# Up's product P6 in two levels beside P5, VectorE's sums regrouped, and k's decay head by head on ScalarE

## The chip, the cores and the metric

The kernel runs on one core of one Trainium2 chip. The metric is the device time of one execution in microseconds (us), the median of several runs. The engines are TensorE (PE: matmuls, PEld: their weight loads), VectorE (DVE), ScalarE (ACT), GpSimd (POOL) and SyncE (SP). POOL and SP issue the transfers here. Each engine works through its own list of instructions in a fixed order, and waits where the next one needs something that is not there yet.

## The reference

```python
for b in range(nb):                    # blocks of 64 positions
    intra = (q_b @ k_b^T * Dmask) @ v_b
    inter = (q_b * lam_pow) @ kv_state
    out[b] = intra + inter
    kv_state = lam**64 * kv_state + (k_b * rev_pow)^T @ v_b
x = out as (3072, 512)                 # (B*S, H*D)
h = x @ w_in                           # (3072, 2048), "Up"
y = (h - tanh(h)) @ w_out              # (3072, 512), "Down"
```

q, k and v are (4, 8, 768, 64), lam has a value per head; everything is float32.

## The kernel before

The kernel takes positions in blocks of 128 and works in six groups (g = 0 to 5). A group is one block of all four batches: 512 tokens. For each group it does attention, then Up (512 to 2048), then Down (2048 to 512). The attention of group g+1 is put between the products of Down of group g.

**Strassen's scheme.** From group 1 on, Up and Down are multiplied by Winograd's form of Strassen's scheme: a matrix product in 2 x 2 quarters takes seven products P1 to P7 of quarters or of sums of quarters (S1 to S4 of the left factor, T1 to T4 of the right one) in place of eight. FACT names the factors: P1 = A11 B11, P2 = A12 B21, P3 = S4 B22, P4 = A22 T4, P5 = S1 T1, P6 = S2 T2, P7 = S3 T3. Each of these may itself be split the same way: "in two levels". Then it is seven products of sixteenths, in the order STEPS = 1, 2, 6, 5, 7, 3, 4.

**Up.** Left factors are weights: w1[u] (quarters and S3) and ws[u] (S1, S2, S4), for u = 0 to 3, each u being 512 of the 2048 columns. up (L540 to L583) does one product for one u in one level: four matmuls of 128x256 (L553). From group GI = 2 on P1, P2 and P5 are done in two levels by inner_steps (L623 to L652): per step four matmuls of 128x128 (L637), one for each u. The right factors' sums come from inner_tokens (L611 to L619, on VectorE at L618), the weights' sums from inner_weights (L601 to L609), which writes them to the DRAM tensor fine_in in group 1; they are read back in pieces of 256 KB. In a two-level product the bank y gathers steps 1, 6, 7 and 4, and is copied out after each of them (L641 by ScalarE, L648 by VectorE), so the next step on y waits for the copy. Steps 5 and 3 share the bank z (L646 copies after step 5), step 2 has w; L651 adds them.

In the up stage, for each u, a bank y is seeded with P1's result by ScalarE (seed, L526 to L529), P6 (L553) is added to it, and it is copied to hidden part 12 (L570); then P7 goes into y (VectorE adds it to part 22 at L574), and P4 last, so y is the sum for part 21. A bank z is seeded with P5's result, and P3 is added to it (L579). finish (L559 to L562) takes the tanh on ScalarE (L561) and subtracts it on VectorE (L562). L582 and L583 make the sums S1 and S3 of Down's left factor, first_sum (L585 to L591) finishes part 11.

**Down.** down_twice (L797 to L841) does a product of Down in two levels: seven steps of four 128x128 matmuls (L811), whose weights come in pieces from the DRAM tensor fine. POOL's queue reads these pieces (L696, and L693 for fine_in) in the order of stream into RING = 7 buffers, so a read waits until TensorE has used the piece seven places earlier. sums_twice (L787 to L795, the operations at L794) makes the left sums on VectorE, L817 the last of them. Copies are at L815 (ScalarE), L824 and L825 (VectorE). sums_once makes Down's S2 (part 11 = S1 - part 11, L739).

**Attention.** att_transpose (L362, L373) works from blocks on VectorE; att_scores (L387, L389, masks L393 on VectorE); att_read (L433), the state's decay on ScalarE (L437); kv_products (L408), which needs k decayed by att_decay (L397 to L399: one VectorE multiplication of 128x512 per batch); att_out (L462, L473, copies L484 on ScalarE, state's addition L482 on VectorE). k itself is loaded by SP (L159) into three buffers.

**Order of a group g >= 2** (L1028 to L1141): the up stage (u = 0 to 3) with Down's P1 spread between; Down's P2; the first half of attention g+1; P4, P5, P6 of Down; the second half; P7; then P3 of Down in turn with P1 and P2 of the next group's Up, then P5 of Up, and P6 for u = 0 and 1. P6 for u = 2 and 3 lies in the up stage. The order written in the source is not yet the order on the engines: a scheduler moves instructions, except where tied or keep_in_program_order holds them.

## Time and profile before

| what | value |
|---|---|
| three runs, median (lowest to highest) | 651.78 us (649.89 to 652.12) |
| the profiled execution, its own time | 650.99 us |
| its span, first to last instruction | 649.2 us |
| matmul records on PE | 6080 |
| P6's first L553 block in groups 2, 3, 4 and 5, by the chain | 269.05, 370.71, 472.09, 572.45 us |
| transfers | 135.79 MB, 209 GB/s over the span |

The profile is of one execution. Times in it are in us from the span's start, durations of single instructions in ns or us as marked. "Idle before" is the time for which an engine waited ahead of the instruction, and the name behind the arrow is what ended the wait. Records of matmuls overlap: the pitch from one to the next, not the duration, is what a matmul costs TensorE. The differences in the row on P6's first block, 101.7, 101.4 and 100.4 us, are the time of a whole group.

### The profile page before, as it was taken

Reading aid. Unit: us, or ns where it says so; the run is one execution under the profiler, and the core shown is the slowest. Engines: PE = TensorE matmul, PEld = TensorE weight load, DVE = VectorE, ACT = ScalarE, POOL = GpSimd, SP = SyncE. Lnnn points to the kernel's source line nnn. Section 1 sums busy time; section 2 is a strip of 40 time slices with the busy share of each in tenths; the row PEclk is TensorE's granted clock in tenths of the full one; section 3 lists DMA queues with packets and bytes.
Section 4 is the critical chain, followed back from the end, with each engine's and each line's share of the span. In section 5 each row is a group of like instructions: output and inputs, shape, how many; then the busy total and the mean of one; then the engine's idle time right before and its main releaser. Section 6 shows DMA issues by size and latency. Waiting matters only on the chain.

```text
span 649.2 us, 15718 instructions
## 1 busy us (share of the span) xinstructions
PE 641.8 (99%) x6080; PEld 594.7 (92%) x6080; DVE 499.2 (77%) x969; ACT 250.2 (39%) x513; POOL 242.6 (37%) x418
## 2 busy tenths in 40 slices
PE   8999999999999999999999999999999999999998
PEld 7888888888888999989999989999998999998997
DVE  4467989958999895778986678998477997485873
ACT  3686765523221222543223453213453313264210
POOL 6000136767756335203435302443411354411341
PEclk9999999999999999999999999999999999999999
DMA  9869987988979858958757967775967686712575
GB/s 201 214 168 206 247 244 233 382 252 231 276 191 268 242 181 253 220 118 220 247 174 226 248 134 160 230 253 199 237 140 158 199 274 210 233 67 66 159 247 162
DMA packets 160281, 135.79 MB, mean 209 GB/s; under 512 B 128640, under 2 KB 130944, under 8 KB 160208
## 3 DMA queue, kind: packets, MB, share of 16 engines
q0 software_dynamic: 30496, 97.88, 47.8%
q1 hardware_dynamic: 128096, 36.53, 26.6%
q8 instruction: 48, 0.79, 0.5%
q10 hardware_dynamic: 1616, 0.39, 0.3%
q14 instruction: 25, 0.20, 0.1%
HBM read 110.10 MB, written 24.64 MB: 208 GB/s over the span
## 4 chain that ended last, share of the span: by engine, by line
PE 91%; DVE 4%; DMA 2%; ACT 1%; issue 1%; ACTq 0%; SPq 0%; DVEq 0%
PE y L811 17%; PE y L553 17%; PE zw L811 13%; PE h L870 8%; PE y L637 7%; PE z L553 6%; PE acc L900 4%; PE z L637 3%; DMA k_nat<-in_k_dram 2%; PE sp L387 2%; PE op L462 2%; PE w L637 2%; PE kv L408 1%; PE op L433 1%; PE end L856 1%; PE op L473 1%
## 5 line engine op out<-in xcount | busy, mean ns | idle before, releaser
L696 POOL DMA_DIRECT2D wb<-fine x204 | 110.1, 540 | 244.0 <-PE y L811 160.8
L815 ACT ACTIVATE q<-y 128x128 f32<-128x128 f32 x112 | 31.1, 277 | 143.2 <-PE y L811 141.7
L811 PE MATMUL y<-wb,g 128*128 128x128 f32 x584 | 76.5, 277 | 0.2 <-DVE tt L618 0.2
L811 PEld LDWEIGHTS y<-wb,g 128*128 128x128 f32 x584 | 70.5, 192 | 1.2 <-issue 0.4
L870 PE MATMUL h<-xt,w 128*128 128x256 f32 x256 | 57.8, 382 | 0.4 <-DVE w L325 0.4
L870 PEld LDWEIGHTS h<-xt,w 128*128 128x128 f32 x256 | 47.6, 190 | 7.8 <-DVE w L325 1.1
L811 PE MATMUL zw<-wb,g 128*128 128x128 f32 x368 | 48.9, 276 | 0.0
L561 ACT ACTIVATE th<-g 128x512 f32<-128x512 f32 x40 | 25.2, 630 | 59.9 <-DVE g L579 42.2
L562 DVE TENSOR_TENSOR g<-g,th 128x512 f32<-128x512 f32 x40 | 27.7, 691 | 24.5 <-ACT th L561 24.4
L811 PEld LDWEIGHTS zw<-wb,g 128*128 128x128 f32 x368 | 44.8, 192 | 0.6 <-DVE g L817 0.6
L553 PE MATMUL y<-xt,w 128*128 128x256 f32 x192 | 45.0, 379 | 0.0
L553 PEld LDWEIGHTS y<-xt,w 128*128 128x128 f32 x192 | 36.4, 190 | 5.1 <-ACT g L570 0.2
L553 PE MATMUL z<-xt,ws 128*128 128x256 f32 x160 | 38.8, 381 | 0.1
L553 PE MATMUL y<-tt,w 128*128 128x256 f32 x160 | 38.3, 382 | 0.0
L811 PE MATMUL zw<-wb,s 128*128 128x128 f32 x280 | 37.9, 275 | 0.0
L553 PE MATMUL y<-tt,ws 128*128 128x256 f32 x160 | 37.8, 379 | 0.0
L811 PE MATMUL y<-wb,s 128*128 128x128 f32 x280 | 37.5, 277 | 0.0
L811 PEld LDWEIGHTS zw<-wb,s 128*128 128x128 f32 x280 | 35.2, 192 | 0.4
L811 PEld LDWEIGHTS y<-wb,s 128*128 128x128 f32 x280 | 34.7, 192 | 0.6
L553 PEld LDWEIGHTS y<-tt,w 128*128 128x128 f32 x160 | 29.8, 190 | 4.7 <-DVE g L574 0.5
L900 PE MATMUL acc<-wt,g 128*128 128x256 f32 x144 | 33.5, 382 | 0.4 <-DVE g L906 0.2
L553 PEld LDWEIGHTS y<-tt,ws 128*128 128x128 f32 x160 | 29.8, 190 | 3.7
(215 smaller groups left out, 1446.0 us busy)
## 6 DMA issues: line engine op xcount, KB each, us to landing
wb<-fine POOLq DMA_DIRECT2D x204, 256.0 KB, 3.8
wb<-fine_in POOLq DMA_DIRECT2D x36, 256.0 KB, 4.4
raw<-in_moe_w_out_dram SPq DMA_DIRECT2D x12, 512.0 KB, 6.2
rest<-fine POOLq DMA_DIRECT2D x20, 256.0 KB, 4.6
raw<-in_moe_w_in_dram SPq DMA_DIRECT2D x16, 256.0 KB, 6.2
fine<-f POOLq DMA_DIRECT2D x16, 256.0 KB, 4.8
q_blk<-in_q_dram SPq DMA_DIRECT2D x128, 32.0 KB, 3.4
k_blk<-in_k_dram SPq DMA_DIRECT2D x128, 32.0 KB, 3.5
```

Source lines behind the costliest of these rows:

```text
L387: tied(g != 1, nc.tensor.matmul(out=sp[j][ts(r, HALF), x:3 + p:2 + p - x, :], lhsT=k0, rhs=qj.rearrange("d (t i) -> d t i", t=2), start=Tr ...
L408: tied(g == 0, nc.tensor.matmul(out=kv[ts(j, 64), n, p, :], lhsT=kd[:, 2 * p + j, :], rhs=vn[:, 2 * p + j, :], start=n == 0 and p == 0, st ...
L462: tied(g == 0, nc.tensor.matmul(out=dst(n, p, j)[:, HALF:BLK], lhsT=vn[:, 2 * p + j, :], rhs=ss[:, j, 2 + p, :], start=g == 0 and n == 0 a ...
L553: nc.tensor.matmul(out=t[:, m, :], lhsT=wt[:, kt, ts(m, 128)], rhs=x[:, kt, :], start=first and m == 0 and kt == 0, stop=kt == 1, skip_gro ...
L561: nc.scalar.activation(th, src, AF.Tanh)
L562: nc.vector.tensor_tensor(dst(c), src, th, op=AL.subtract)
L637: nc.tensor.matmul(out=dst[:, ts(u, 128)], lhsT=a, rhs=b, start=x in (1, 2, 5) and u == 0, stop=True, skip_group_check=True)
L696: nc.gpsimd.dma_start(out=t.rearrange("p m c -> p (m c)"), in_=fine[TWICE.index(n_), SUB.index(x_)].rearrange("p u c -> p (u c)"))
L811: tied(x == STEPS[-1], nc.tensor.matmul(out=dst, lhsT=a[:, u, :], rhs=wb[:, ts(u, 128)], start=x in (1, 2) and u == 0, stop=u == NU - 1, s ...
L815: nc.scalar.activation(keep, dst, AF.Copy)
L870: tied(u == 0, nc.tensor.matmul(out=hm[c][:, m, :], lhsT=w1[u][:, i, a, ts(m, 128)], rhs=xt[0, t][:, i, :], start=m == 0 and i == 0, stop= ...
L900: nc.tensor.matmul(out=acc[n][:, r, :], lhsT=a[:, ts(r, 128)], rhs=b, start=kt == 0 and r == 0, stop=kt == KH - 1, skip_group_check=True)
```

## The change

P6 of Up joins P1, P2 and P5 in two levels (INNER has 6). The sums of its weights are made by 16 VectorE operations at the end of group 1 (inner_weights in the loop over STEPS, into the dead buffer of group 1's S1 part) and written to fine_in. Its tokens' sums are made in each group by inner_tokens. Its steps alternate with those of P5, its result lands in the hidden part 21 (dead at that time), and a new function second_sum adds it to P1's result on VectorE for each u; only then is y seeded. So the up stage has only P3, P7 and P4 left; the order of these is written anew, with the seeds of u = 2 and 3 behind P4 of u = 0 and 1, and L570 is not run any more from group 2 on.

In Down, S2 (sums_once(g, 11, ...)) and P1's sums are moved: S2 stands behind the first half of attention and P2's results (every(p2)), P1's sums behind up(0, 7). More operations are held in program order (L408, L433, L739 from group 2 on), fewer elsewhere (seeds and L641, L646).

att_decay from group 3 on is done by ScalarE: eight operations of 128x64 per batch, each with the head's column of the mask as a per-partition scale.

On the engines the scheduler makes this of it in groups 2 to 5, from the crossing on. TensorE: fourteen blocks of P5 and P6 in turn, two matmuls of Down's P1, P3 and P7 of u = 0, half of P7 of u = 1, then one matmul of P4 of u = 0, P3 of u = 1, and so on. VectorE: the four second sums, then 36 operations up to the last P4's subtraction; behind P2's and P4's sums come the four masks, the state's addition, the three o11 additions and only then the four L739 differences. ScalarE, where it has the decays: b = 0 and 1 between the tanh operations of the up stage; b = 2 (eight) between the state's decay and the two copies L484; b = 3 (four and four) behind the first and the second copy of Down's P4.

```diff
-    fine_in = dram.tile([3, 3, 128, NU, 128], F32, name="fine_in")
+    fine_in = dram.tile([4, 3, 128, NU, 128], F32, name="fine_in")
     w_in_u = moe_w_in.rearrange("k (a n) -> k a n", a=2)
...
         kp = raw[g, b]["k"].rearrange("s (p j) d -> s p j d", j=2)
+        if g > GI:
+            for h in range(H):
+                p, j = divmod(h, 2)
+                nc.scalar.activation(kp[:, p, j], kp[:, p, j], AF.Copy, scale=mask[:, j, 2 + p, HALF - 1:HALF])
+            return None
         return tied(g != 1, nc.vector.tensor_tensor(kp, kp, bwd, op=AL.mult))
...
                 for j in range(2):
-                    tied(g == 0, nc.tensor.matmul(out=kv[ts(j, 64), n, p, :], lhsT=kd[:, 2 * p + j, :],
+                    tied(g == 0 or g >= GB, nc.tensor.matmul(out=kv[ts(j, 64), n, p, :], lhsT=kd[:, 2 * p + j, :],
                                                   rhs=vn[:, 2 * p + j, :], start=n == 0 and p == 0, stop=True,
...
                         for pp in (p, p + 2):
-                            nc.tensor.matmul(out=out_dst(ops, n, pp, j), lhsT=state[r, b, pp, :],
-                                             rhs=tr[g, b][2][r, pp, :], start=n == 0 and p == 0, stop=False,
-                                             skip_group_check=True)
+                            tied(g >= GB, nc.tensor.matmul(out=out_dst(ops, n, pp, j), lhsT=state[r, b, pp, :],
+                                                           rhs=tr[g, b][2][r, pp, :], start=n == 0 and p == 0, stop=False,
+                                                           skip_group_check=True))
             for p in (3, 2, 1, 0):
...
         banks[key, x] = bank(x, tag, 1)
-        tied(x == "y" and key[2] < 2, nc.scalar.activation(banks[key, x].rearrange("q (m c) -> q m c", m=2), src, AF.Copy))
+        tied(False, nc.scalar.activation(banks[key, x].rearrange("q (m c) -> q m c", m=2), src, AF.Copy))
...
     def seed_up(g, u):
-        seed(("up", g, u), "y", ("yb", "w", "ya")[u % 3], hidden(g, 12)[:, u])
+        seed(("up", g, u), "y", ("w", "yb", "ya")[u % 3], hidden(g, 12)[:, u])
+    def second_sum(g, u):
+        nc.vector.tensor_tensor(hidden(g, 12)[:, u], hidden(g, 12)[:, u], hidden(g, 21)[:, u], op=AL.add)
...
         key = ("up", g, u)
-        if g >= GI and n == 6 and u > 1:
-            seed_up(g, u)
-        if g >= GI and n == 3:
+        if g >= GI and n in (3, 7) and (key, "z") not in banks and (n == 3 or u > 1):
             seed(key, "z", "z", hidden(g, 22)[:, u])
...
             finish(12, dst(12))
-        if n == (3 if g < GI else 7):
+        if n == (3 if g < GI or u > 1 else 7):
             nc.vector.tensor_tensor(dst("S1"), dst(12), dst(22), op=AL.add)
...
-    INNER = (1, 2, 5)
+    INNER = (1, 2, 5, 6)
     toks = {}
...
     def a_quarter(n, u, i, k):
-        return (ws[u][:, 0, k] if n == 5 else w1[u][:, 2 * n - 2 + k, 0])[:, ts(i, 128)]
-    def inner_weights(u, ns=INNER):
+        return (ws[u][:, n - 5, k] if n > 2 else w1[u][:, 2 * n - 2 + k, 0])[:, ts(i, 128)]
+    def inner_weights(u, ns=INNER[:3]):
         for n in ns:
             a11, a12, a21, a22 = (a_quarter(n, u, i, k) for i in range(2) for k in range(2))
-            t = late["pool"].tile([128, 4, 128], F32, name="ws2", tag="sums", bufs=6)
+            if n < 6:
+                t = late["pool"].tile([128, 4, 128], F32, name="ws2", tag="sums", bufs=6)
+            else:
+                t = hidden(GI - 1, "S1")[:, u].rearrange("p m c -> p (m c)").rearrange("p (x c) -> p x c", x=4)
             s1, s2, s4 = (t[:, x] for x in range(3))
...
                 tc.keep_in_program_order(nc.vector.tensor_tensor(dst, x, y, op=op))
-            (nc.sync if u == NU - 1 else nc.gpsimd).dma_start(out=fine_in[INNER.index(n)].rearrange("x p u c -> p u x c")[:, u], in_=t[:, 0:3])
-    def inner_tokens(g):
-        for n in INNER:
+            (nc.sync if u == NU - 1 and n < 6 else nc.gpsimd).dma_start(out=fine_in[INNER.index(n)].rearrange("x p u c -> p u x c")[:, u], in_=t[:, 0:3])
+    def inner_tokens(g, ns):
+        for n in ns:
             x = xt[g][FACT[n][1]]
...
-        tags = {1: ("yb", "att", "att"), 2: ("w", "att", "att"), 5: ("ya", "att", "z")}[n]
+        tags = {1: ("yb", "att", "att"), 2: ("w", "att", "att"), 5: ("ya", "att", "z"), 6: ("yb", "att", "att")}[n]
         y, w, z = (bank(x, tag, 4 if tag == "att" else 1) for x, tag in zip(("y3", "w3", "z3"), tags))
         r5 = otile("r5")
-        out4 = hidden(g, {1: 12, 2: 11, 5: 22}[n])
+        out4 = hidden(g, {1: 12, 2: 11, 5: 22, 6: 21}[n])
         c11, c12, c21, c22 = (out4[:, :, i, ts(j, 128)] for i in range(2) for j in range(2))
...
             if x in (1, 4, 6):
-                op = tied(n == 5, nc.scalar.activation({1: c11, 4: c21, 6: c12}[x], d, AF.Copy))
+                op = tied(False, nc.scalar.activation({1: c11, 4: c21, 6: c12}[x], d, AF.Copy))
                 if (n, x) == (1, 6) and g < NG - 1:
...
             elif x == 5:
-                tied(n == 5, nc.scalar.activation(r5, dst, AF.Copy))
+                tied(False, nc.scalar.activation(r5, dst, AF.Copy))
             elif x == 7:
...
                 yield from ((g + 1, ("in", n), x) for n in (1, 2))
-        yield from ((g + 1, ("in", 5), x) for x in STEPS if x in (3, 5, 6))
+        yield from ((g + 1, ("in", n), x) for x in STEPS if x in (3, 5, 6) for n in (5, 6))
...
     def sum_once(g, u, dst, x, y):
-        tied(dst == 21, nc.vector.tensor_tensor(hidden(g, dst)[:, u], hidden(g, x)[:, u], hidden(g, y)[:, u], op=AL.subtract))
+        tied(g >= GI, nc.vector.tensor_tensor(hidden(g, dst)[:, u], hidden(g, x)[:, u], hidden(g, y)[:, u], op=AL.subtract))
...
         p0, p1 = attention(g + 1) if not last else ([], [])
-        if g < GI:
-            p_first = down(g, 1)
-        else:
-            sums_twice(g, 1)
-            p_first = down_twice(g, 1)
+        p_first = down(g, 1) if g < GI else down_twice(g, 1)
         for u in range(NU):
...
             else:
-                up(g, u, 3)
-                up(g, u, 7)
-                if u + 2 < NU:
-                    up(g, u + 2, 6)
-                else:
-                    next(p_first)
-                up(g, u, 4)
-                if u + 1 == NU:
+                for w_, n in {0: ((0, 3), (0, 7), (1, 3), (0, 4)), 1: ((1, 7),), 2: ((1, 4), (2, 7), (2, 3), (2, 4)),
+                             3: ((3, 7), (3, 3), (3, 4))}[u]:
+                    up(g, w_, n)
+                    if (w_, n) == (0, 7):
+                        sums_twice(g, 1)
+                    if (w_, n) == (1, 7) or (w_, n) == (3, 3):
+                        steps(p_first, 2 if w_ == 1 else 1)
+                    if n == 4 and w_ + 2 < NU:
+                        seed_up(g, w_ + 2)
+                if u == NU - 1:
                     sums_twice(g, 2)
-                if u != 2:
-                    steps(p_first, (2, 1, 0, 2)[u])
+                steps(p_first, (0, 0, 2, 2)[u])
                 if not last and u < 2:
...
             sums_twice(g, 4)
-            sums_once(g, 11, "S1", 11)
             p2 = down_twice(g, 2)
...
         if g >= GI:
+            sums_once(g, 11, "S1", 11)
             sums_twice(g, 5)
...
             steps(p4, 4)
-            inner_weights(NU - 1, INNER[2:])
+            inner_weights(NU - 1, INNER[2:3])
         every(p4)
...
             continue
-        inner_tokens(g + 1)
+        inner_tokens(g + 1, INNER[:3])
         sums_twice(g, 3)
-        p3, pa, pb, pc = (down_twice(g, 3), *(inner_steps(g + 1, n) for n in INNER))
-        for _ in STEPS:
+        p3, pa, pb, pc, pd = (down_twice(g, 3), *(inner_steps(g + 1, n) for n in INNER))
+        for i, _ in enumerate(STEPS):
             next(p3)
...
             next(pb)
+            if g == GI - 1 and i < NU:
+                inner_weights(i, INNER[3:])
         for p in (pa, pb, p3):
             every(p)
+        inner_tokens(g + 1, INNER[3:])
         for x in STEPS:
-            if x == STEPS[-1]:
-                up(g + 1, 0, 6)
             next(pc)
-            if x in (7, 3):
-                seed_up(g + 1, int(x == 3))
+            next(pd)
             if x in (1, 6, 7):
...
         every(pc)
+        every(pd)
         first_sum(g + 1, 3)
-        up(g + 1, 1, 6)
+        for u in range(NU):
+            second_sum(g + 1, u)
+            if u < 2:
+                seed_up(g + 1, u)
```

## Prediction

> **What bounds the kernel now.** I began with the page's busy times and its 40 slices.
>
> ```profile
> PE 641.8 (99%) x6080; PEld 594.7 (92%) x6080; DVE 499.2 (77%) x969; ACT 250.2 (39%) x513; POOL 242.6 (37%) x418
> PE   8999999999999999999999999999999999999998
> PEclk9999999999999999999999999999999999999999
> ```
>
> TensorE (PE) works 641.8 of 649.2 us at the full granted clock. Only fewer or shorter matmuls, or the few small holes between them, can give anything. I then asked for stretches of group 2: the up stage, the end of Up and P2 of Down, and Down's P4 to P6; the last row is the up stage of group 5. Columns: stretch, length, busy time of PE, PEld, VectorE (DVE), ScalarE (ACT), POOL, clock, DMA share, GB/s.
>
> ```profile
> 269.00:303.45 34.45, 34.34 (x187) 30.71 (x186) 26.88 (x43) 14.78 (x27) 5.37 (x10) 1.00 0.72 154
> 303.45:310.50 7.05, 7.05 (x65) 7.03 (x63) 7.05 (x13) 1.11 (x4) 4.17 (x8) 1.00 0.90 290
> 315.70:334.70 19.00, 19.00 (x168) 18.83 (x168) 18.63 (x38) 4.13 (x13) 9.20 (x17) 1.00 0.72 225
> 572.40:606.60 34.20, 34.20 (x187) 30.58 (x186) 22.46 (x35) 14.82 (x27) 3.22 (x6) 1.00 0.18 53
> ```
>
> TensorE is full in each; VectorE is the second bound, at 78% in the first row and 98 to 100% in the two below it. ScalarE has room. Third, the chain that ended last, in order of time (start, us, what), where group 2 of Up begins:
>
> ```profile
> 245.59 1.79 PE y L637 x16
> 265.25 0.95 PE y L637 x8
> 267.09 0.95 PE y L637 x8
> 268.05 1.00 PE z L637 x8
> 269.05 1.73 PE y L553 x8
> ```
>
> A matmul of this kernel leaves two records. Sixteen records of 128 columns take 1.79 us, 0.112 each; eight of 256 columns take 1.73, 0.216 each. So a block of four small matmuls needs 0.893 us. The blocks of P5 alone show 0.95, 0.95 and 1.00: holes of 0.06, 0.06 and 0.11, because P5's own copies hold it. Elsewhere in this stretch the starts of the matmuls leave 0.3 us of holes, mostly before the last P4. Hence the kernel has about 0.5 us to win per group besides the arithmetic.
>
> **The change, part by part.** It acts in groups 2 to 5, four times.
>
> 1. *P6 in two levels.* Out: four blocks of eight 256-column records, 4 x 1.73 = 6.91 us. In: seven blocks of 0.893, 6.25 us. 0.66 us less per group, **2.6 us in all**. Blocks of just this shape stand in the chain above, so no bound is open here.
>
> 2. *The crossing into Up.* P5's and P6's blocks alternate, so each copy lies beside the other's block and the 0.22 us of holes go. But before, P6's one-level blocks lay between P5's end and the first P3, and covered its copies; now they don't. Hops come from the time line (start, us, engine):
>
> ```profile
> 263.30 1.06 PE L637 MATMUL y<-tt,ws 128*128 128x128 f32 x8
> 264.39 0.60 ACT L641 ACTIVATE g<-y 128x512 f32<-128x512 f32 x1 [0.30 <-PE y L637]
> 269.69 0.68 DVE L589 TENSOR_TENSOR g<-g,g 128x512 f32<-128x512 f32 x1
> 270.47 0.63 ACT L590 ACTIVATE th<-g 128x512 f32<-128x512 f32 x1 [1.62 <-DVE g L589]
> 271.13 0.69 DVE L591 TENSOR_TENSOR g<-g,th 128x512 f32<-128x512 f32 x1 [0.76 <-ACT th L590]
> ```
>
> A block issued from 263.30 to 264.19 is copied from 264.39: 0.20 later. DVE to ACT is 0.10, ACT to DVE 0.03; to PE I take 0.10. Three links follow each other. (a) After P5's last block: 0.20, copy 0.60, seed of z 0.59 (L529), hops 0.13, together 1.52; beside it lie P6's last block 0.89 and two P1 matmuls 0.45. TensorE waits 0.18. (b) After P6's last block: 0.20, 0.24 until ScalarE is free of that seed, copy 0.60, the new second sum on VectorE 0.69, seed of y 0.60, hops 0.26: 2.59. Beside it lie 0.45, the wait of (a) and the first P3, 1.73: 2.36. It waits 0.2. (c) P4 may overwrite y once VectorE has added P7: 0.20 + 0.68 + 0.10 = 0.98 against two matmuls of the next P7, 0.86: 0.1. The sum is 0.5; after a wait the trace often loses another 0.1 on the second record (an eight-record block that began at 300.57 took 1.99 instead of 1.89). I take 0.7, bounded by 0.3 and 1.3 (none, or one and a half, of these extras). Less the 0.22 that goes: 0.5 per group, **+2.0 us**, bounds +0.3 and +4.3.
>
> 3. *More for VectorE.* Per group three additions to P6's results and four second sums (seven of 0.684, L648 and L651) and four token sums of 0.282 (L618): 5.9 us; the weight sums of group 1's end, sixteen of 0.282, fall into a VectorE pause from 250.9 to 257.3 and cost nothing. From P6's last block to the first P2 block TensorE now has 27.5 us of work (twelve Up blocks of 1.73, seven P1 blocks of 0.893, the waits above); VectorE has 40 operations there. Three independent ones take 1.89 us (L589), so one starts every 0.605: 24.2 us, 88%. P2 needs the last P4's tanh and subtraction: 0.20 + 0.60 + 0.69 + hops 0.15 = 1.64 against two P1 blocks, 1.79. The cover holds by 0.15 where the queue is short; I charge 0.1 in groups 2 to 4, none in 5, which has no transposes: **+0.3 us**. Bounds: 0, and +8.5 if each of some 36 queued operations costs its full 0.684 (36 x 0.079 = 2.8 in three groups).
>
> 4. *S2 and the four L739 differences behind the masks.* Before, they stand ahead of the masks in the stretch that is 7.05 of 7.05 busy; now they follow the state's addition and o11, 2.4 us later. P4's subtraction for x = 3 moves from 318.3 to about 319.4, ends at 320.1 and is wanted at 320.1. 0.1 in three groups, **+0.3 us**, bounds 0 and +0.9. The stretch to 334.7 gains these 2.4 and loses three P7 sums and, in two groups, two decays of 0.684: no net.
>
> 5. *k's decay on ScalarE*, for groups 3 and 4: 32 heads each, on 128x64. No row has this shape. The state's decay has the same kind of scale:
>
> ```profile
> 312.89 1.28 ACT L437 ACTIVATE state<-state,fwd 128x128 f32<-128x128 f32 x4 [1.89 <-PE op L433]
> 315.75 1.08 ACT L484 ACTIVATE xt<-op 128x512 f32<-128x512 f32 x2 [1.58 <-PE op L473]
> 316.82 0.28 ACT L815 ACTIVATE q<-y 128x128 f32<-128x128 f32 x1
> ```
>
> L437 lasts 0.391, four take 1.28, so 0.296 apart. A column costs (0.597 - 0.277)/384 = 0.83 ns (L641 against L815), so 64 columns: 0.338, and 0.243 apart; bounds 0.24 and 0.39 per head. In Up (16 heads) ScalarE is 43% busy and nothing near them is wanted soon: nothing; if that cover goes, up to 3 us in a group. Batch 2's eight stand between L437 and the two xt copies: 314.07 + 1.95 = 316.0, xt to 317.1, P4's first copy q to 317.4, and P4's third block wants it at 317.5. Batch 3's k is loaded from 313.7 (2.3 to 4.4 us to land), its first four heads wait behind that first copy, for the load's first part only, and the next copy is wanted near 319.2. I charge 0.2 in two groups, **+0.4 us**, bounds 0 and +3.2.
>
> The Trainium skill (ScalarE: Activation LUTs, "What ACT_TABLE_LOAD costs") gives 186 ns plus 0.833 ns a column, about 93 ns more for a per-partition scale, and a 93 ns overlap back to back: 332 ns and 239 ns for 64 columns as an estimate, and 386 for L437's 128, where the trace has 391. Its "Rules for kernel authors" say that multiplying belongs on VectorE; by that rule the decays get dearer, which is rival D.
>
> 6. *Transfers.* Three more 256 KB reads of S2's rows per group, 0.75 MB beside 21 (209 GB/s over 101 us): hidden. At the first crossing the rows are written first: last sum done by about 254.2, POOL's turn near 256, write 3.0 (fine_in, POOL), issue 0.5, read 4.4, so they are in by 264; P6's third block wants them at 267.8. Nothing; POOL's queue behind it (reads for P1) has until 275.8.
>
> **Sum.** -2.6 + 2.0 + 0.3 + 0.3 + 0.4 = +0.4 us. The profiled execution took 650.99 (span 649.2 and 1.8 around it), so **651.4 us**, 0.4 below the median of 651.78: no change.
>
> **Rivals.**
> A, the forecast: the arithmetic is paid back at the crossing. Own range 649.6 to 653.2. Chance 0.51.
> B, links (a) to (c) cost no more than the 0.22 that go, because hops are shorter than I take, and the rest is hidden: 650.99 - 2.6 = 648.4. For it: the three waits are short beside the chains that make them. Against it: all three chains are wanted at once. 0.20.
> C, slower: VectorE becomes the bound between the second sums and P2. It decides from a pitch of about 0.61 us, where the cover of 0.15 is used up; the price is 1.4 us a group in three groups at half of the bound above: 655.7. For it: 98 to 100% just after; against it: 88% in the stretch. 0.14.
> D, ScalarE's queue: at 0.338 a head without overlap, eight take 2.7 us, q ends near 318.1, P4 waits 0.7 and again 0.7 behind batch 3: 651.4 + 2.8 = 654.2. The L437 row, 1.28 for four, speaks against it. 0.10.
> E, it does not do what it says: S2's rows come late at the first crossing, once, by some 3 us: 654.4. 0.05.
>
> A measurement of this kernel can tell about 0.5% (3.3 us) from no change: under 648.5 is faster, over 655.0 slower. B lies on the lower border (0.08 faster, 0.12 within); C gives 0.10 slower, D and E 0.02 each, A 0.01. So faster 0.08, same 0.77, slower 0.15. The range 648.4 to 655.5 leaves out some 0.08 below and 0.07 above.
>
> **What would show it.** Step 1: seven L637-like blocks more of 0.893 per group and four L553 blocks fewer. Step 2: holes before the first z block, the first and second y blocks of each group, 0.1 to 0.3 each. Step 3: no hole over 0.3 before the first P2 block. Step 4: P4's x = 3 starting within 0.2 of its turn. Step 5: a head's decay of 0.34 and 0.24 apart, P4's third block on time. The forecast is wrong if holes at the crossing are absent, or if one elsewhere in a group passes 1 us.

## The result, and the profile after

| kernel | median of its runs | lowest to highest | ratio to before, 95% interval |
|---|---|---|---|
| before | 651.52 us (13 runs) | 649.89 to 654.14 | |
| changed | 654.84 us (13 runs) | 652.43 to 658.21 | 1.0049, 1.003 to 1.0068 |

The changed kernel is slower by 3.3 us, 0.49%: inside the bounds of the forecast's range (648.4 to 655.5), but the forecast was no change, and the sum of the steps (+0.4 us) is wrong. The ratio is made from the single executions; here and below it is not the quotient of the two medians. The profiled execution took 654.61 us, its span is 652.8.

The page's busy times and the chain's shares of the changed kernel:

```profile
PE 641.5 (98%) x6176; PEld 594.9 (91%) x6176; DVE 512.0 (78%) x1021; ACT 264.0 (40%) x577; POOL 251.6 (39%) x434
PE 86%; DVE 6%; issue 3%; DMA 2%; ACT 2%; POOL 0%; ACTq 0%; DVEq 0%; POOLq 0%
```

TensorE is busy for nearly the same time as before (641.8) in a span that is 3.6 us longer, so the loss is time in which it stands. (The busy time does not show the arithmetic won: a record of L811 lasts 0.277 at a pitch of 0.112, so that holes under 0.16 are counted as busy.) "issue" has grown from 1% to 3% of the chain: time in which an engine waited for nothing that the profile shows. Of it, 6.79 us stand in one piece at 97.04, ahead of the stretches that follow. And 1.1 of the 3.6 us lie before the first score matmul of group 1 (207.99 before, 209.10 now), where the kernel before alone spreads from 207.99 to 209.50 (e12).

To find where, I cut both profiles at the first score matmul of each half of the attention, and asked for these stretches. Columns as in the prediction (length, then PE, PEld, DVE, ACT, POOL busy, clock, DMA share, GB/s). Before, from the second half in group 1 to the second half in group 4:

```profile
233.63:310.64 77.01, 76.90 (x701) 72.80 (x700) 59.04 (x105) 29.84 (x62) 24.23 (x44) 1.00 0.78 197
310.64:334.86 24.22, 24.22 (x365) 23.62 (x364) 23.32 (x47) 5.68 (x18) 9.88 (x18) 1.00 0.71 219
334.86:412.02 77.16, 77.16 (x717) 73.24 (x716) 57.96 (x100) 29.89 (x62) 23.20 (x42) 1.00 0.76 198
412.02:436.24 24.22, 24.22 (x365) 23.62 (x364) 23.32 (x47) 5.68 (x18) 10.93 (x20) 1.00 0.71 224
436.24:513.66 77.42, 77.42 (x717) 73.38 (x716) 56.79 (x98) 29.98 (x62) 24.26 (x44) 1.00 0.73 189
513.66:537.38 23.72, 23.51 (x333) 22.87 (x332) 21.49 (x43) 5.69 (x18) 12.02 (x22) 1.00 0.75 249
```

The same of the changed kernel:

```profile
235.18:313.04 77.86, 77.50 (x737) 73.36 (x736) 62.73 (x122) 33.44 (x78) 28.86 (x52) 1.00 0.79 209
313.04:338.47 25.43, 24.28 (x361) 23.72 (x360) 22.70 (x46) 9.50 (x34) 9.87 (x19) 1.00 0.71 234
338.47:416.03 77.56, 77.27 (x737) 73.28 (x736) 59.54 (x106) 33.41 (x78) 25.82 (x48) 1.00 0.80 207
416.03:440.18 24.15, 24.15 (x361) 23.64 (x360) 22.36 (x45) 9.26 (x34) 9.88 (x19) 1.00 0.73 228
440.18:517.13 76.95, 76.95 (x737) 73.11 (x736) 59.80 (x108) 29.70 (x62) 25.83 (x48) 1.00 0.78 201
517.13:541.21 24.08, 23.59 (x329) 22.86 (x328) 22.47 (x45) 5.68 (x18) 10.72 (x21) 1.00 0.65 218
```

The 77 us stretches hold a crossing into Up, the up stage and P2; the 24 us ones hold P4 to P6 of Down and one half of the attention at their start. In group 4 (the fifth row) the new crossing is 0.47 us faster and TensorE is full in it: the arithmetic is won there. The first rows do not hold the same work: before has 16 matmul records fewer in it and 16 more in the stretch ahead of it. The largest loss stands in the second row: 25.43 us with only 24.28 busy, in a stretch whose matmuls the change does not touch. TensorE's time line in it (in brackets: idle before, and what ended it):

```profile
316.42 1.10 PE L468 MATMUL op<-ss,v_nat 128*64 128x64 f32 x32
317.45 0.46 PE L479 MATMUL op<-ss,v_nat 64*64 64x64 f32 x14
319.06 0.56 PE L479 MATMUL op<-ss,v_nat 64*64 64x64 f32 x18 [1.15 <-issue]
319.54 1.16 PE L821 MATMUL y<-wb,g 128*128 128x128 f32 x8
```

In the middle of 32 equal records (L479, L473 before) TensorE stands for 1.36 us over its pitch. The masks it needs had ended at 315.96, and the view names no semaphore that ended the wait. Two more such waits, of 0.57 and 0.50 us, stand in the first row (at 240.28) and in the third (at 343.85); without its own the third row would be 0.10 us faster than before.

**The records behind "issue".** TensorE's list has 12,665 records in the trace (6176 matmuls, 6176 weight loads, 313 semaphores and the like; before 12,452). A DMA queue of the kind "instruction" brings 49 packets of 16 KB (48 before), about one for 256 records. The pages' lines of it, before and changed (packets, MB, share of the DMA engines):

```profile
q8 instruction: 48, 0.79, 0.5%
q8 instruction: 49, 0.80, 0.5%
```

I numbered the records and looked at every gap over 0.2 us that nothing explains: in this profile after 100 us they stand at records 4290, 5826 and 6594, in that of before at 3522 alone (0.21 us). All leave the remainder 194 when divided by 256 (the rest, below), and each ends 1.2 to 1.7 us after such a packet landed. So TensorE had run to the border of a page of its program and the next page was not there: this is read from the place and the timing, and e7 and e8 below test it. In the attention it gets through 391 records in 5.0 us, a page in about 3.3; in blocks of 0.893 a page lasts 14 us, and there no such gap is seen, but for some just behind a half.

The Trainium skill (Runtime: NRT & Kernel Launch, "Instruction fetch mechanics") has the blocks of 16 KiB and 256 instructions, and the trace agrees. It holds the fetch to be mostly hidden, and gives TensorE a store of 2048 instructions; by that hardly a page could be late, and here the measurement decides: at these stalls the page is used 1.2 to 1.7 us after its landing.

**What the change has to do with it.** A group is 2254 records in the changed kernel and 2198 before (48 more of P6, 8 more semaphores). So the borders fall elsewhere from group 2 on: in group 2's halves on record 356 and 381 of 391, where before they fell on 151 and 179. A border late in a half has a page behind it that was all attention, and so the shortest time for the fetch. That this is what makes a page late is argued, not shown: in e7 and e10 below, borders on records 228 and 159 of a half were hit too.

The stalls differ from one execution to the next, so I add them up by profile: gaps over 0.1 us at these records after 100 us, beside the time from the first score in group 1 to the last matmul.

| profile | time from there | stalls at page borders | without them |
|---|---|---|---|
| before | 438.02 | 0.21 | 437.81 |
| before, e12 | 439.25 | 0.70 | 438.55 |
| changed | 440.58 | 2.42 | 438.16 |
| changed, e1 | 439.54 | 0.95 | 438.59 |
| changed and mended, e5 | 442.10 | 4.03 | 438.07 |
| changed and mended, e18 | 439.12 | 1.24 | 437.88 |

Without the stalls both the two profiles of before and the four of the changed kernel come to 438.18 in the mean. With them the changed ones are 1.7 us longer. Four profiles are few for sums that go from 0.95 to 4.03. All thirteen profiles here with the longer list and the borders left alone have 0.2 to 4.0 us of stalls, 1.6 in the mean; the three with the list of before (with e3) have 0.2, 0.7 and 0.7. By these the difference is about 1 us.

### The profile page after: what moved, and what is told of

It is laid out like the page before. It is cut to its first block, busy times and chain, and to the rows that moved or that the text cites. A ratio compares the mean times of both kernels' runs of the same rounds, so it can differ in the third digit from the quotient of the medians.

```text
span 652.8 us, 16075 instructions
## 1 busy us (share of the span) xinstructions
PE 641.5 (98%) x6176; PEld 594.9 (91%) x6176; DVE 512.0 (78%) x1021; ACT 264.0 (40%) x577; POOL 251.6 (39%) x434
## 3 DMA queue, kind: packets, MB, share of 16 engines
HBM read 113.25 MB, written 25.43 MB: 212 GB/s over the span
## 4 chain that ended last, share of the span: by engine, by line
PE 86%; DVE 6%; issue 3%; DMA 2%; ACT 2%; POOL 0%; ACTq 0%; DVEq 0%; POOLq 0%
PE y L821 17%; PE y L560 13%; PE zw L821 13%; PE y L647 9%; PE z L560 7%; PE h L880 6%; PE z L647 4%; PE acc L910 4%; PE w L647 2%; PE op L468 2%; PE sp L387 1%; PE kv L414 1%; PE op L479 1%; PE end L866 1%; DMA q_nat<-in_q_dram 1%
## 5 line engine op out<-in xcount | busy, mean ns | idle before, releaser
L651 ACT ACTIVATE g<-y 128x512 f32<-128x512 f32 x48 | 28.6, 595 | 31.0 <-PE y L647 31.0
L703 POOL DMA_DIRECT2D wb<-fine_in x48 | 25.8, 540 | 26.8 <-PE zw L821 9.5
L560 PEld LDWEIGHTS z<-xt,ws 128*128 128x128 f32 x160 | 30.1, 190 | 4.6 <-ACT z L535 0.7
L393 DVE TENSOR_TENSOR ss<-sp,mask 128x384 f32<-128x384 f32 x48 | 23.7, 549 | 13.0 <-PE sp L389 13.0
```

The lines of the kernel that those rows point to most:

```text
L393: op = tied(g != 1, nc.vector.tensor_tensor(ss[:, j], sp[j], mask[:, j], op=AL.mult))
L560: nc.tensor.matmul(out=t[:, m, :], lhsT=wt[:, kt, ts(m, 128)], rhs=x[:, kt, :], start=first and m == 0 and kt == 0, stop=kt == 1, skip_gro ...
L651: op = tied(False, nc.scalar.activation({1: c11, 4: c21, 6: c12}[x], d, AF.Copy))
L703: nc.gpsimd.dma_start(out=t.rearrange("p m c -> p (m c)"), in_=fine_in[INNER.index(n_[1]), (5, 6, 3).index(x_)].rearrange("p u c -> p (u c)"))
```

## The experiments

Each was timed against the kernel before on the same chip (before's medians there: 652.54, 652.26, 652.16, 651.32 and 652.49 us for e1 to e4, e5 to e8, e9 to e12, e13 and e14, e15 to e18).

| run | median us | ratio, 95% interval |
|---|---|---|
| e1 changed, again | 655.30 | 1.0033, 1.0009 to 1.0056 |
| e2 P6 alone | 654.52 | 1.0050, 1.0022 to 1.0077 |
| e3 all but P6 | 657.47 | 1.0063, 1.0038 to 1.0088 |
| e4 decay on VectorE | 657.11 | 1.0069, 1.0043 to 1.0095 |
| e5 mended in group 1 | 653.47 | 1.0025, 1.0009 to 1.0041 |
| e6 the same, a P1 block earlier | 656.28 | 1.0055, 1.0036 to 1.0073 |
| e7 changed, pages moved by 128 | 657.60 | 1.0068, 1.0038 to 1.0098 |
| e8 before, pages moved by 60 | 653.54 | 1.0010, 0.9994 to 1.0027 |
| e9 e5 without S2's writes | 653.41 | 1.0005, 0.9982 to 1.0028 |
| e10 e5, pages moved by -60 | 654.59 | 1.0023, 0.9995 to 1.0050 |
| e11 e9 and e10 | 653.72 | 1.0012, 0.9986 to 1.0038 |
| e12 before, again | 652.08 | 0.9989, 0.9962 to 1.0016 |
| e13 e5, S2's writes unread | 653.67 | 1.0031, 1.0010 to 1.0053 |
| e14 e5, S2's writes by ScalarE | 655.21 | 1.0067, 1.0042 to 1.0092 |
| e15 e13, writes four times | 659.03 | 1.0106, 1.0089 to 1.0122 |
| e16 e13, writes of 1.5 KB | 654.78 | 1.0030, 1.0012 to 1.0048 |
| e17 e9 without S2's reads | 653.62 | 1.0027, 1.0011 to 1.0044 |
| e18 e5, again | 656.16 | 1.0060, 1.0038 to 1.0082 |

e5 and e18 are one kernel in two calls and lie 0.35% apart, with intervals that hardly overlap. So a difference under 0.35% (2.3 us) between two rows decides nothing by itself, and for smaller ones I go by the gaps in the profiles.

**The clock behind a long wait.** For each execution the granted TensorE clock is on record, and executions at 0.997 or less are mostly 2 to 4 us longer than others of the same kernel. Three profiles show where that comes from. After 100 us, TensorE stands for 1.91 us in e2, 2.17 in e10 and 3.02 in e15, and behind each of these waits the clock row gives 0.50 for 3.4 us; behind none of the waits up to 1.79 (e7) does it. (A wait of 1.95 in group 0 of e14 had none behind it.) In e2 eight records then take 1.91 us in place of 1.06; the last line is the stretch, with the clock ahead of the DMA share:

```profile
308.62 0.77 PE L815 MATMUL zw<-wb,s 128*128 128x128 f32 x2 [1.91 <-DVE k_nat L399]
309.18 1.91 PE L815 MATMUL y<-wb,s 128*128 128x128 f32 x8
312.10 1.06 PE L815 MATMUL y<-wb,g 128*128 128x128 f32 x8
308.60:312.00 3.40, 3.38 (x16) 3.40 (x17) 3.40 (x6) 0.28 (x1) 0.54 (x1) 0.50 0.83 296
```

3.4 us at half the clock are 1.7 us of work, or 0.997 over an execution. So by these figures a wait near 2 us costs nearly twice its length. In e18, 6 of 9 executions are at 0.997 or less, in e5 1 of 12. By the means of the executions at 0.999 and 1.0 alone, the changed and mended kernel is 2.46 (e1), 1.18 (e5) and 1.88 us (e18) above before, and e5 and e18 are 0.1% apart.

**e1: the changed kernel again.**

> The changed kernel once more, for a second profile. Theory I (TensorE's issue): of the 3.3 us by which the changed kernel is slower, most is time in which TensorE waits inside the short matmuls of the attention for nothing that the profile shows (gaps over 0.25 us add up to 10.5 us in the profiled execution against 5.2 before, 1.36 of it inside one L479 block at 317.7); if it belongs to the code, the gaps at 317.7 and 343.3 stand at the same places again, if it is a chance of one execution, at others. Rival X (crossing): the holes at the crossing into Up (0.58 us per group) and P4's x = 3 (up to 0.76) are dearer than the arithmetic won; they stand again, and the issue gaps do not. Both expect 654 to 656 us.

The gap at 343 stood again (at 341.6, 0.59, same record), that at 317 hardly (under 0.05), and a wait of 0.80 for P2's weights came at 310.8. So the place belongs to the code and the size to the execution.

**e2 to e4: the parts.** e2 has the old lines for S2 and k's decay; e3 is the kernel before with the new ones; e4 takes out only this:

```diff
-        if g > GI:
-            for h in range(H):
-                p, j = divmod(h, 2)
-                nc.scalar.activation(kp[:, p, j], kp[:, p, j], AF.Copy, scale=mask[:, j, 2 + p, HALF - 1:HALF])
-            return None
```

> The changed kernel with Down's S2 and the differences L749 back at their place before P2, and k's decay back on VectorE: only P6 in two levels and the new order of Up are left. Rival X (crossing): the crossing sets the loss, so 654 to 655. Rival S (the moves): S2's place or the decay on ScalarE brings the loss, so 651 to 652. Theory I: the added matmuls shift where TensorE's code is refilled, so gaps in the attention stay and the time is 653 to 655.

> The kernel before with Down's S2 behind the masks and k's decay on ScalarE, but P6 in one level and the old order of Up. Rival X: no loss, 651 to 652. Rival S: the whole loss, 654 to 655. Theory I: TensorE's list of matmuls is that of before, so no new issue gaps and 651 to 652.5.

> The changed kernel with k's decay back on VectorE, S2 left where the change has it. If the decay on ScalarE costs what step 5 took (+0.4 us), 654.4; if ScalarE's queue is the loss (rival D of the prediction), 652; if VectorE's load is what hurts, it gets worse by up to 2 us, 656.5. Theory I: 654 to 655.

None of the three is better than the whole. P6 alone (e2) waits once 2.07 us in group 2's P2 (ended by k's decay L399 on VectorE, as the view has it; the piece of weights had landed only at 308.49, just before the wait ended at 308.62, so it may be the read). All but P6 (e3) waits 1.47 in group 3 for the copy q, which stands behind the decays on ScalarE: rival D's mechanism, once. With TensorE's list as before, e3 should have come to 651 to 652.5 by theory I; it came to 657.47 with only 0.7 us of stalls at page borders, so S2 and the decays without P6 have costs of their own, of which this wait is the one shown. With the decay back on VectorE TensorE waits in Down, from 300 to 530:

```profile
PE zw L815 <- DVE g L821: 1.6, 3, 0.8
PE zw L815 <- DVE q L829: 1.3, 1, 1.3
```

That is rival C's bound: with P6's sums VectorE has no room for k's decays, and e4 is 2.3 us slower than e1 of the same call by the ratios, just the bound named above; the two rows bear out 2.9 in its profile. So by these waits the decay on ScalarE does not cost; it pays for what P6's sums add on VectorE.

**e5 and e18: a slip in group 1.** In the changed kernel four L749 differences lost their fixed place in group 1 too, since the condition became g >= GI, and they stand ahead of k's decay and the masks.

```diff
-        tied(g >= GI, nc.vector.tensor_tensor(hidden(g, dst)[:, u], ...
+        tied(g >= GI or dst == 21, nc.vector.tensor_tensor(hidden(g, dst)[:, u], ...
```

> The changed kernel with one condition mended: the differences into part 21 (L749) are held in program order in group 1 as well (g >= GI or dst == 21). In the changed kernel these four lost their place in group 1 and stand ahead of k's decay and the masks: gaps of 0.77 ahead of L414 and twice 0.31 inside L468 near 211 to 214. Theory T (this slip is part of the loss): those three gaps go, 0.8 to 1.2 us faster than the changed kernel. Rival: the time is taken back by the next wait, so under 0.3 us.

> The kernel of e5 once more, on the same chip as the three above, as their measure: a ratio of 1.0025 within 0.2%. Theories T, I and Q leave it there.

The three gaps (0.77, 0.31, 0.31) went, and one of 0.80 came near 232, where TensorE waits for L827 on VectorE. The stretch between group 1's halves is 25.60 in e1 and 25.36 in e18 (in e5 26.65, of which 1.28 is a stall at a page border): 0.24 us, so the rival was right, and as a main cause this theory falls.

**e6: a P1 block earlier.**

```diff
-                steps(p_first, (0, 0, 2, 2)[u])
+                steps(p_first, (1, 0, 1, 2)[u])
```

> As before it, and one of the two P1 blocks (Down) at the end of u = 2 moved to the end of u = 0, so that TensorE uses the first piece of weights earlier and POOL can read ahead. Theory Q (late reads): in group 2 P2's pieces are read in a bunch with k and v from 301 on, land after 3 to 5 us instead of 2.3 to 2.8, and P2's blocks wait up to 2 us; with the block moved the reads spread out, these waits fall by half or more, and the time falls by 0.5 to 1.5 us against the run before it. Rival: the reads wait for other buffers than P1's, so nothing moves.

P2 still waited, 1.61 us at 307.9, and a new gap of 0.32 stands between two blocks on bank y, in three groups. So moving a P1 block did not take away the lateness of P2's weights, as theory Q expected.

**e7 and e8: move the pages.** Tiny matmuls at the start, 32 on the changed kernel, 15 on the kernel before:

```diff
     idle_products(8, True)
+    for _ in range(32):
+        nc.tensor.matmul(out=idle[0:64, 0:64], lhsT=fwd[0:64, 0, 0:64], rhs=fwd[0:64, 0, 0:64], start=True, stop=True)
```

> The changed kernel with 32 tiny matmuls (64x64) on the unused idle bank at the start, where TensorE waits for loads anyway: they compute nothing that is used, and move the borders of TensorE's code pages by 128 records against its work. Theory I (code pages): all stalls of the kind 'issue' lie at record numbers with the same rest (193 or 194) by 256, some 1.2 to 1.6 us after a 16 KB code page landed; so the gaps at 239.7, 317.7 and 343.3 (records 331, 356 and 381 of an attention half) go or shrink, since the border falls on records 203, 228 and 253; new ones can come only in group 3, on records 278 and 303. 0.5 to 1.5 us faster than the changed kernel. Rival: the stalls belong to the instructions (L479, L468) or to the data, so they stay where they are.

> The kernel before with 15 such matmuls, which move the borders by 60 records, on to records 347 and 375 of group 2's two attention halves, 318 of group 1's second and 302 of group 4's first. Theory I: gaps of the kind 'issue' appear there, which the kernel before does not have, 0.2 to 1.4 us each, and the time rises by 0.5 to 2 us. Rival: the stalls come from what the change does to the transfers or to the queues, so none appears here and the time stays within 0.3 us of before.

This tells the two theories apart. TensorE's time line of e8, the kernel before with nothing else changed, in group 2 and in group 4 (L475 is L473):

```profile
315.20 0.44 PE L475 MATMUL op<-ss,v_nat 64*64 64x64 f32 x10
316.38 0.57 PE L475 MATMUL op<-ss,v_nat 64*64 64x64 f32 x22 [0.73 <-issue]
...
518.45 0.56 PE L475 MATMUL op<-ss,v_nat 64*64 64x64 f32 x20
520.20 0.45 PE L475 MATMUL op<-ss,v_nat 64*64 64x64 f32 x12 [1.18 <-issue]
```

The same place in e12, the kernel before itself:

```profile
316.02 1.04 PE L462 MATMUL op<-ss,v_nat 128*64 128x64 f32 x30
316.99 0.69 PE L473 MATMUL op<-ss,v_nat 64*64 64x64 f32 x32
317.62 1.16 PE L811 MATMUL y<-wb,g 128*128 128x128 f32 x8
```

Stalls of 0.95 and 1.39 stand where the moved borders lie (records 5826 and 10177, rests 194 and 193), in two of the places foretold; the two others stayed empty. In e7 all three old gaps went, and new ones came at records 5825, 8898 and 10434, again with rests 193 and 194: 1.98 in L416 and 0.42 in L470, and 1.03 in a block of P4 just behind a half. The second was foretold, the first not: a border on record 228 of a half can still be hit. So the stalls follow the page border, not the instruction and not the change. Nor are they made by the added transfers: e8 has none, and e17, where none are left, has 1.9 us of such stalls. The time tells less: e8 is 0.65 us above before by the ratio, with no change inside its interval, and 1.1 by the executions at 0.999 and 1.0; what its fillers cost of that is not shown. e7's fillers took 7.0 us at the start (64 records of 0.11; e8's 30 records 1.9), so its time says nothing of the rest.

**e10 and e11: move them back.** The fillers of the start are issued in pieces of up to 512 columns, 15 matmuls less; e11 also leaves out what e9 leaves out.

```diff
-        for _ in range(n):
-            tied(not first, nc.tensor.matmul(out=idle[:, 0:128], lhsT=fwd[:, 0, :], rhs=fwd[:, 0, :], start=True, stop=True))
+        while n > 0:
+            x = min(n, 4)
+            tied(not first, nc.tensor.matmul(out=idle[:, 0:128 * x]..., lhsT=fwd[:, 0, :],
+                                             rhs=fwd[:, 0:1, :].to_broadcast([128, x, BLK]), start=True, stop=True))
+            n -= x
```

> The changed kernel with the condition mended as in e5, and the filler matmuls of the start (idle products, whose result is not used) issued as fewer and wider ones, 15 matmuls less for the same columns. That moves the borders of TensorE's code pages by 60 records the other way, to about records 160 and 185 of group 2's halves, 210 and 235 of group 3's, 98 of group 4's second: the places where the kernel before has them. Theory I: no gap of the kind 'issue' over 0.3 in groups 2 to 5 (e5's profile has 1.36 and 0.90 in group 2), at most one each in group 1's halves (records 365 and 391 of 391): 0.5 to 1.5 us faster than e5. Rival: the gaps stay in group 2's L479.

> Both of the above: mended condition, moved code pages, and no writes of P6's weight sums (P6's part of the result is left out in the same way). If the three causes T, I and Q are the whole loss, the time comes to what the prediction had for the rest, 651.4 on a profile of 650.99 before, so 0 to 0.8 us above the kernel before of the same call; if the crossing or the ScalarE decay has a loss of its own, 1.5 us or more stays.

e10 is 0.2% under the mean of e5 and e18, e11 0.1% under the mean of e9, e13, e16 and e17: the sign that theory I wants, but below what the rows can tell. By the executions at 0.999 and 1.0, e10 is 1.6 us above before, no better than e5 and e18 (1.2 and 1.9). e11's profile has 0.98 us of stalls at borders where e9's has 2.16. e10's own profile, of its longest execution (663.3 us, clock 0.992) and so a weak witness, goes against theory I, which expected no issue gap over 0.3 in groups 2 to 5: it has 2.43 us at record 5569, the largest after 100 us in all runs, besides 0.62 at record 7874 and 0.38 at 4289:

```profile
321.57 0.81 PE L442 MATMUL op<-qd,state 64*64 64x128 f32 x18 [2.17 <-issue]
```

The border lay on record 159 of the half, near the 151 of before, but the packet began only 7.8 us after TensorE had passed the border before it (in the changed kernel's three stalls 1.7 to 2.4). So a page is also late when its fetch begins late, and the border's place alone does not decide; why it began late is open. The expected 0.5 to 1.5 us is not shown.

**e9, e13 to e17: S2's transfers.** In the changed kernel the first read of P6's rows waits until all four writes have landed. POOL in the changed kernel (last column: idle before):

```profile
258.64 0.78 POOL L619 DMA_DIRECT2D fine_in<-gS  x1
265.69 2.68 POOL L703 DMA_DIRECT2D wb<-fine_in  x5 [6.27 <-PE y L647]
```

POOL stands for 6.3 us with five reads and a result write behind it. TensorE, which the view names, is not what it waited for alone, since in e13, where no read waits for these writes, the reads go one by one:

```profile
255.89 0.78 POOL L619 DMA_DIRECT2D fine_in<-gS  x1
256.65 1.11 POOL L703 DMA_DIRECT2D wb<-fine_in  x2
259.31 0.54 POOL L703 DMA_DIRECT2D wb<-fine_in  x1 [1.55 <-PE zw L821]
260.20 0.54 POOL L703 DMA_DIRECT2D wb<-fine_in  x1 [0.35 <-PE z L647]
```

The edits, all on e5's kernel: e9 skips the write for n == 6 and reads P5's rows, e13 keeps the write and reads P5's rows, e14 has (nc.scalar if n == 6 else ...).dma_start and reads as e5 does. On top of e13, e15 writes four times and e16 one partition of 128; on top of e9, e17 takes P5's pieces for P6 and has no such reads. All but e14 leave out P6's part of the result. Here e9's two edits:

```diff
+            if n == 6:
+                continue
...
-                    INNER.index(n_[1]), (5, 6, 3).index(x_)]
+                    min(INNER.index(n_[1]), 2), (5, 6, 3).index(x_)]
```

> The changed kernel with the condition mended as in e5, and without the four writes of P6's weight sums by POOL: P6 reads the rows of P5's sums instead of its own, so its part of the result is left out and one that means nothing stands in its place; reads, matmuls and sums stay as many. Theory Q (the first crossing's transfers): the writes stand in POOL's queue ahead of reads and slow SP's loads of q, k and v for group 3, which end at 306 instead of 301 and then meet P2's weights in group 2; without them SP's last load is issued 2 to 4 us earlier, P2's waits in group 2 (0.5 to 2 us in the profiles) go, and the time falls by 0.5 to 1.5 us against e5's 653.5. Rival: the three added reads and the new order of Up do it, so nothing moves.

> The kernel of e5 with the four writes of P6's weight sums still issued by POOL, but P6 reads the rows of P5's sums, so no read waits for these writes (P6's part of the result is left out, as in e9). Theory Q1 (the wait): what costs in e5 is that the first read of P6's rows waits in POOL's queue until all four writes have landed (POOL stands from 258.7 to 265.3), with four more reads and a result write behind it, which then go out in one bunch; here the reads go out at 259 to 263 as in e9, and the time is that of e9, 0.5 to 1.5 us under e5. Theory Q2 (the bytes): the 0.75 MB written, or POOL's waits for VectorE's sums, are the cost; then it stays at e5's ratio of 1.0025.

> The kernel of e5 with these four writes issued by ScalarE's queue instead of POOL's; the whole result is computed. Theory Q1: the writes go out earlier and the first read waits 2 to 4 us less, so a part of Q comes back: 0.3 to 1 us under e5, a ratio of about 1.001. Rival: ScalarE waits for VectorE's sums in its own queue and P5's and P6's copies stand behind, so the crossing into group 2 gets holes of 0.5 to 2 us and it is no faster than e5.

> The kernel of e13 with each of the four writes of P6's weight sums issued four times (to rows that nobody reads): the suspected cost made four times as large, 2.9 MB instead of 0.75. P6's part of the result is left out as in e13. Theory Q2 (the bytes, and POOL's time for issuing them): 2 to 4 us slower than e13 (ratio 1.006 to 1.009). Rival: the writes themselves cost nothing and e9's lower time was spread; then within 0.2% of e13.

> The kernel of e13 with the four writes cut to one partition, 1.5 KB each: POOL still waits for VectorE's sums before each, but hardly a byte is moved. P6's part of the result is left out. Theory Q2 by bytes: the time of e9 (1.0005); by POOL's waits: the time of e13 (1.0031). Rival (spread only): no difference between e13, this and e18 of this call.

> The kernel of e9 (no writes), and P6 takes P5's pieces of weights that are already on the chip, so that the twelve added reads of 256 KB are gone as well (P6's part of the result is left out): the change's matmuls, sums and order, without any added transfer. If the transfers cost nothing beyond the writes (step 6 of the prediction), the time of e9; if the reads cost too, 0.5 to 1.5 us less. If what is left over the kernel before is the crossing and step 5, about 1.000 to 1.001.

Four times the writes are dear: e15 is 0.75% above e13 (five executions) and waits once for a piece of weights at the crossing, with half the clock for 3.4 us behind it:

```profile
263.71 1.62 PE L822 MATMUL zw<-wb,g 128*128 128x128 f32 x6 [3.02 <-DMA wb<-fine]
```

The bytes of the change itself are not: e16, with hardly a byte, equals e13, and e17, with no added transfer, equals both. e9's low ratio looked like a gain of 1.3 us and was not borne out by e11, e16 and e17. The five runs without the wait have a mean of 1.0021, the four mended or changed ones (first measurement, e1, e5, e18) 1.0042; that is 1.4 us, at the edge of the spread. In the profiles, without stalls at borders, they stand at 437.9 (e9), 437.4 (e13), 438.6 (e16) and 437.8 (e17) against 438.2, so about 0.3. By the executions at 0.999 and 1.0 it is 0.3 too: the five are 1.6 above before in the mean, e1, e5 and e18 1.8. ScalarE as the issuer is no help (e14, 1.0067); its profile shows no hole of TensorE at that crossing, so its rival, holes there, was not seen, and what makes its time is not shown.

**e12: before again.**

> The kernel before, unchanged, as a control: a ratio of 1.000 within 0.2%, and in its profile no gap of the kind 'issue' over 0.3 in groups 2 to 5 and no wait for P2's weights in group 2, if the first profile of it was no chance.

0.9989, as expected, and no issue gap over 0.3 in groups 2 to 5. In group 0 it has stalls of 0.99 and 1.85 at records 450 and 705, like most profiles here: there the code is the same in all kernels.

## Why the prediction was wrong, by its own steps

1. *P6 in two levels, -2.6 us.* Right. The chain of waits of the changed kernel shows the blocks at the forecast price, 1.79 for two and 3.57 for four (0.893 each):

```profile
264.61 3.57 PE y L647 x32
...
277.12 1.79 PE y L647 x16
278.91 0.45 PE y L821 x4
279.35 1.98 PE z L560 x8
```

2. *The crossing, +0.5 a group.* The links were right, though not in every size: 0.14 and 0.10 at the first z, 0.04 and 0.10 at the first y, 0.08 and 0.10 at P4 of u = 0, alike in groups 2 to 4, 0.58 where I had 0.7. The account was not: with P6's blocks not only the 0.22 at the crossing went, but also 0.2 to 0.4 of holes in the rest of the up stage before (0.10 and 0.10 near 395.8 and 402.0 in group 3, 0.17 and 0.10 near 603.8 in group 5). So it costs about 0.1 a group, not 0.5.
3. *VectorE, +0.3.* No wait ahead of the first P2 block; the cover held. P2's later steps wait for copies, 0.42 a group in groups 2 to 4 where before had 0.07 to 0.25: some 0.8 in all, where I had 0.3. And e4 shows that the cover holds only because of step 5. Steps 1 to 3 together, in group 4's stretch: 77.42 became 76.95.
4. *S2 behind the masks, +0.3.* The size was right by luck, as the place was not: nothing in groups 2 and 3, 0.66 in group 4, where the half has no kv products and P4's x = 3 comes sooner; that stretch went from 23.72 to 24.08.
5. *The decay, +0.4.* The price was right: 0.334 each, eight in 2.00, so 0.238 apart (I had 0.338 and 0.243; the estimate from the Trainium skill, ScalarE: Activation LUTs, "What ACT_TABLE_LOAD costs", was 332 and 239 ns, and the trace agrees). In group 2's Down the xt copies behind it waited for TensorE's stall and not for the decays (first two lines). In group 3's Down, without a stall, they came right behind the decays (last two lines), some 0.3 after the last L479; yet P4's blocks there keep their pitch of 0.89 from the second on, so no cost of the step shows on TensorE.

```profile
316.53 2.00 ACT L403 ACTIVATE k_nat<-k_nat,mask 128x64 f32<-128x64 f32 x8
319.58 1.09 ACT L490 ACTIVATE xt<-op 128x512 f32<-128x512 f32 x2 [1.05 <-PE op L479]
419.52 2.01 ACT L403 ACTIVATE k_nat<-k_nat,mask 128x64 f32<-128x64 f32 x8
421.43 1.05 ACT L490 ACTIVATE xt<-op 128x512 f32<-128x512 f32 x2
```

The Trainium skill's rule (ScalarE: Activation LUTs, "Rules for kernel authors") that multiplying belongs on VectorE does not hold here: moving it back made the kernel slower (e4).
6. *Transfers, 0.* Nearly right: e16 and e17 found no cost over the spread, though POOL stood 6.3 us where I had it free, and the reads that wait for the writes landed from 269.0 on, not by 264.

Without the stalls the profiles come to a difference of 0.0 (438.18 in both) where the sum of the steps was +0.4. That is close by luck: the crossing was charged some 1.6 us too much, step 3 some 0.5 too little and step 5 0.4 too much, so by the measured sizes the steps should have won about 1 us. In the first profile most of this is lost ahead of group 2's attention (104.0 us from group 1's first score, 102.6 before, 0.57 of the difference a stall); where it went in the others is not shown.

**The step that failed is the sum itself: it has no term for TensorE's supply of instructions.** I wrote that a hole over 1 us elsewhere in a group would show the forecast wrong, and it stands at 317.7, in the attention, which I took for unchanged. P6's two levels and their semaphores make the list longer by 56 records a group, so the pages' borders moved from records 151 and 179 to 356 and 381 of group 2's halves. The stalls of four profiles (2.2 us in the mean) less those of two before (0.5) are 1.7 us, all that these profiles differ by.

That the stalls stand at page borders, and move with them, is shown by e7 and e8. That the borders' new places make the changed kernel's loss is argued: moving them back (e10, e11) changed the time by less than the spread, and by more profiles the difference of the stalls is nearer 1 us. Of the 2.7 us of the timed runs (the mean ratio of 1.0042), a part is the clock: by the executions at 0.999 and 1.0 alone it is 1.8 us (e1, e5 and e18). Whether long stalls at borders brought those lower clocks is not shown, as all four profiles of the changed and mended kernel have full clock. So the cause of the whole loss stays open in part. Of the rivals, C and D exist as mechanisms (e4, e3) but not in the whole change; B was nearest for the crossing, and E did not happen. No mended version beats the kernel before.

## What to carry to other kernels

Where the pacing engine rushes through many short instructions, count them: a change that only makes its list longer moves the page borders into other places, and the stalls there can cost what it wins. An "issue" wait in the middle of equal instructions is read by numbering the records: a common rest by the page size tells the program from the data. And when two edits load one engine and unload it again, as P6's sums and k's decay do here, cost them together. Before two timings are compared, look at the granted clock of the single executions: one long wait can cost its length and then a stretch at half the clock.

## What the runs showed of the hardware that was not expected

- TensorE's program comes in pages of 16 KB, 256 records. A late page stalls it for 0.2 to 2.4 us (after the first 100 us), ending 1.2 to 1.7 us after the packet landed; one page of attention work is 3.3 us.
- The size of such a stall varies from under 0.05 to 1.36 us at one record of one program (317.7 in the changed kernel's two profiles).
- After 100 us, each wait of TensorE of 1.91 us or more (1.91, 2.17 and 3.02 in e2, e10 and e15) had 3.4 us at half the granted clock behind it, and none up to 1.79 had.
- A filler of 64x64 took 0.063 us a record in a row of 30 at the start (e8) and 0.11 in a row of 64 (e7). In e7 the score records behind it are slow too (0.47 at 14.54 where e8's take 0.32), so a lower clock at the start is likely; the windows of the profile do not show it.
